# A rational activation's denominator as (|h| + c)|h| in one operation, its scale moved to where sums leave PSUM, and a new order of issue

## The chip, the core and the metric

One core of a Trainium2 chip runs the whole program in one launch. The core has TensorE (PE; its loads of weights are listed as PEld), VectorE (DVE), ScalarE (ACT) and GpSimd (POOL), each with its own row of instructions that it works off in order, and SyncE (SP), which issues the DMAs. SBUF holds operands, PSUM takes the sums of matmuls. The metric is the device time of the core in microseconds (us), the median of several runs.

## The reference

Windowed attention with block summaries, then a network with a rational activation, then a second network (relu6):

```python
def _attn_ref(q, k, v):            # 2 batches, 8 heads, 768 positions, 64 wide
    k_sum = k.reshape(B, H, nb, block, D).max(axis=3)       # block 32
    v_sum = v.reshape(B, H, nb, block, D).mean(axis=3)
    scores_l = scale * np.matmul(q, k.transpose(0, 1, 3, 2))
    mask_l = np.abs(pos[:, None] - pos[None, :]) < window   # 16
    scores_s = scale * np.einsum('bhsd,bhnd->bhsn', q, k_sum) + np.log(block)
    ...                                                     # softmax over both, times v and v_sum

def _moe_ref(x, w_in, w_out, a, b):   # 1536 x 512, 512 x 2048, 2048 x 512
    h = x @ w_in
    P = a[0] + a[1] * h + a[2] * h2 + a[3] * h3
    Q = 1.0 + np.abs(b[0]) * np.abs(h) + np.abs(b[1]) * h2
    g = P / (Q + 1e-06)
    return g @ w_out

def _moe2_ref(x, w_in, w_out):
    h = x @ w_in
    return (h * np.clip(h + 3.0, 0.0, 6.0) / 6.0) @ w_out
```

## The kernel before

**Stages.** The attention runs in twelve groups of 128 positions (six for each batch). A group has scores on PE (`L507`), which DVE takes out of PSUM with the mask and a running extreme (`L520`), the exponential on ACT (`L534`), sums (`L538`), a guard (`L546`), a reciprocal (`L552`), the share (`L549`, `L555`), transposes on PE (`L574`) that are copied out by ACT or DVE (`L577`, `L578`), the product with v (`L591`), and two halves of its result for the first network: a rounded one (`L601`, `L602`) and the rest (`L603`, on DVE). `L376` on DVE forms the block maxima of k; `L432` and `L434` form the block means of v on PE.

The first network takes 1536 positions as three chunks of 512 and the 2048 inner columns as two halves of eight slices of 128, that is 48 steps. A step is a first product (`L637`, twelve matmuls, since each operand is a rounded part and a rest), the activation `act1`, a `low` operation (`L745`, the rest of g) and a second product (`L654`, twelve matmuls into the four banks y_81 to y_84). The first sixteen steps are single, 512 columns wide, and lie beside the attention's second half; the other thirty-two run in sixteen pairs, 1024 wide. After eight steps `evac` takes the four sums out of PSUM (`L667` on ACT or `L668` on DVE the first time, `L672` the second). The second network follows (`L812`, `L850`, `L865`, `L939` and others).

**Weights** come in as 512 KB pieces by DMA (`raw`, `L280`), and are brought into a rounded part and a rest by a row of operations on several engines: a clamp (`L305`), ACT (`L309`), a shift (`L311`), an or (`L313`), a cast (`L286` on ACT, `L322` on DVE) and a subtraction (`L325`).

**The activation before.** `act1` puts |h| into q (`L701`, ACT), forms u = |b1||h| + |b0| on POOL, ACT or DVE (`L704`, `L707`), multiplies q by u on POOL or DVE (`L717`), so that q + 1 + 1e-6 is the denominator. The numerator runs on ACT (`L721`) and DVE (`L723`, `L724`). An approximate reciprocal r comes from Ln and Exp on ACT (`L728`, `L730`), is used by `L733`, corrected by `L735` and `L737`, all on DVE; `L739` on ACT rounds the result and `L745` on DVE or POOL forms its rest. u is a single buffer, shared by all steps; in a single step r stands in u, in a pair in PSUM.

**What sets the order.** All operations are recorded in a plan first. Where an operation has forms on several engines, a digit of the string `PICK` chooses. The string `ORDER` then gives one order of all operations, and each engine gets its own in that order; nothing is reordered after that. Where the planner sees PE idle for more than 0.6 us it puts filler matmuls on a bank that is free (`L1045`); at the start sixteen such matmuls on a zero tile z stand in the code (`L349`).

**Names.** hs_91 to hs_94 are four PSUM banks; attention groups from the fifth on have their scores and products in hs_93 and hs_94, and single steps have theirs in hs_91 and hs_92. raw_70 to raw_73 are buffers for raw weights, t_74, t_75, q_76, q_77, u the tiles of the activation (early groups and early weights borrow them), xx_115 and xx_117 chunks of the first network's input, ab the tile of the coefficients a and |b|.

## Time and profile before

| what | value |
|---|---|
| median of 3 runs | 589.26 us (588.09 to 589.53) |
| span of the profiled execution | 587.4 us |
| PE busy | 578.6 us, 98% |
| DVE busy | 494.4 us, 84% |
| ACT busy | 348.5 us, 59% |
| POOL busy | 294.7 us, 50% |
| chain that ended last, on PE | 94% |

The span runs from the first to the last instruction of one execution; the time of a run is 589.26 - 587.4 = 1.86 us longer here. Busy time is what an engine's operations took; an average over the whole says little, so the rows below cut the program into the stretch ahead of the first network (0 to 38 us), the single steps (38 to 150), the pairs (150 to 323) and the second network. In a row of groups the mean time of one operation stands behind the busy time, and then the time that its engine was idle just before it, with what ended most of that. In a chain of waits each piece was waited for by the next.

### The profile page before, as it was taken

Reading aid. Unit: us, or ns where it says so; the run is one execution under the profiler, and the core shown is the slowest. Engines: PE = TensorE matmul, PEld = TensorE weight load, DVE = VectorE, ACT = ScalarE, POOL = GpSimd, SP = SyncE. Lnnn points to the kernel's source line nnn. Section 1 sums busy time; section 2 is a strip of 40 time slices with the busy share of each in tenths; the row PEclk is TensorE's granted clock in tenths of the full one; section 3 lists DMA queues with packets and bytes.
Section 4 is the critical chain, followed back from the end, with each engine's and each line's share of the span. In section 5 each row is a group of like instructions: output and inputs, shape, how many; then the busy total and the mean of one; then the engine's idle time right before and its main releaser. Section 6 shows DMA issues by size and latency. Waiting matters only on the chain.

```text
span 587.4 us, 9645 instructions
## 1 busy us (share of the span) xinstructions
PE 578.6 (98%) x3608; PEld 466.6 (79%) x3613; DVE 494.4 (84%) x887; ACT 348.5 (59%) x648; POOL 294.7 (50%) x272
## 2 busy tenths in 40 slices
PE   8999999999999999999999999999999999999997
PEld 4477788888888888888888888888888888888886
DVE  5999999999989898988899998968687786866643
ACT  3988998988676677658657455524540434424410
POOL 1777676573475657654766472131423175523210
PEclk9999999999999999999999999999999999999999
DMA  8986534301222223110000141320313023002005
GB/s 311 352 306 209 192 118 151 104 30 35 73 71 73 76 101 110 37 36 2 17 20 1 37 143 37 107 73 0 144 32 113 1 73 126 18 0 73 1 1 214
DMA packets 17983, 53.10 MB, mean 90 GB/s; under 512 B 2273, under 2 KB 2785, under 8 KB 17937
## 3 DMA queue, kind: packets, MB, share of 16 engines
q1 hardware_dynamic: 17936, 52.49, 26.1%
q8 instruction: 28, 0.46, 0.3%
q14 instruction: 19, 0.15, 0.1%
HBM read 48.55 MB, written 3.15 MB: 88 GB/s over the span
## 4 chain that ended last, share of the span: by engine, by line
PE 94%; DMA 2%; DVE 1%; SPq 1%; issue 1%; POOL 0%; ACT 0%; DVEq 0%
PE y L654 23%; PE y L850 22%; PE hb L637 15%; PE hc L812 13%; PE hs L637 8%; PE hc L939 7%; PE hs L591 2%; PE hs L507 2%; PE hs L574 1%; DMA mask_sb<-in_masks 1%; DMA k<-in_blk 1%; SPq L280 1%; DVE s L520 0%; POOL s L549 0%; PE hs L434 0%
## 5 line engine op out<-in xcount | busy, mean ns | idle before, releaser
L654 PE MATMUL y<-g,wt 128*128 128x512 f32 x576 | 139.1, 392 | 0.0
L654 PEld LDWEIGHTS y<-g,wt 128*128 128x128 f32 x576 | 106.8, 188 | 22.3 <-POOL g L745 0.3
L850 PE MATMUL y<-wt,g 128*128 128x512 f32 x480 | 116.1, 389 | 0.0
L850 PEld LDWEIGHTS y<-wt,g 128*128 128x128 f32 x480 | 90.1, 188 | 18.7
L637 PE MATMUL hb<-xx,wt 128*128 128x512 f32 x384 | 89.5, 389 | 0.0
L325 POOL TENSOR_TENSOR wt<-raw,wt 128x512 fp32r<-128x512 f32 x44 | 62.4, 1425 | 51.0 <-DVE wt L322 30.4
L637 PEld LDWEIGHTS hb<-xx,wt 128*128 128x128 f32 x384 | 72.1, 188 | 15.0
L309 ACT ACTIVATE raw<-raw 128x512 f32<-128x512 f32 x62 | 41.1, 676 | 33.3 <-POOL raw L305 24.6
L717 POOL TENSOR_TENSOR q<-q,u 128x512 f32<-128x512 f32 x34 | 46.2, 1368 | 23.8 <-ACT u L707 14.4
L828 POOL TENSOR_TENSOR g<-t,g 128x512 fp32r<-128x512 f32 x17 | 23.4, 1380 | 63.3 <-ACT g L825 63.3
L825 ACT ACTIVATE g<-t 128x512 fp32r<-128x512 f32 x40 | 25.0, 628 | 49.4 <-PE y L850 43.4
L305 POOL TENSOR_SCALAR raw<-raw 128x512 f32<-128x512 f32 x44 | 35.8, 815 | 34.1 <-DMA raw<-in_w 33.9
L286 ACT ACTIVATE wt<-raw 128x512 fp32r<-128x512 f32 x56 | 36.8, 671 | 25.7 <-POOL raw L796 6.6
L313 DVE SCALAR_TENSOR_TENSOR raw<-raw 128x512 int32<-128x512 int32 x62 | 47.7, 779 | 4.3 <-ACT raw L309 4.1
L637 PE MATMUL hs<-xx,wt 128*128 128x512 f32 x192 | 47.8, 398 | 0.0
L812 PE MATMUL hc<-wt,wt 128*128 128x512 f32 x192 | 47.4, 389 | 0.0
L745 POOL TENSOR_TENSOR g<-t,g 128x512 fp32r<-128x512 f32 x22 | 30.6, 1397 | 30.3 <-ACT g L739 25.8
L939 PE MATMUL hc<-xx,wt 128*128 128x512 f32 x192 | 45.6, 389 | 0.0
L865 DVE SCALAR_TENSOR_TENSOR part<-y,part 128x512 f32<-128x512 f32 x36 | 24.4, 684 | 22.1 <-PE y L850 22.0
L939 PEld LDWEIGHTS hc<-xx,wt 128*128 128x128 f32 x192 | 36.0, 188 | 7.5
L812 PEld LDWEIGHTS hc<-wt,wt 128*128 128x128 f32 x192 | 36.0, 188 | 7.5
L637 PEld LDWEIGHTS hs<-xx,wt 128*128 128x128 f32 x192 | 35.1, 188 | 7.7 <-issue 0.2
(175 smaller groups left out, 1097.6 us busy)
## 6 DMA issues: line engine op xcount, KB each, us to landing
raw<-in_w SPq DMA_DIRECT2D x62, 512.0 KB, 4.2
vv<-in_vw SPq DMA_DIRECT2D x6, 512.0 KB, 7.1
out<-part SPq DMA_DIRECT2D x12, 256.0 KB, 2.9
k<-in_kT SPq DMA_DIRECT2D x4, 384.0 KB, 3.7
q<-in_qT SPq DMA_DIRECT2D x6, 256.0 KB, 7.5
e<-in_kT SPq DMA_DIRECT2D x4, 384.0 KB
raw<-in_vt SPq DMA_DIRECT2D x3, 512.0 KB, 5.1
e<-in_vw SPq DMA_DIRECT2D x3, 512.0 KB
```

Source lines behind the costliest of these rows:

```text
L286: nc.scalar.activation(out_, in_, AF.Copy)
L305: eng.tensor_scalar(out=hif, in0=hif, scalar1=CAP, scalar2=-CAP, op0=ALU.min, op1=ALU.max)
L309: add(ACT, 0.58, lambda: nc.scalar.activation(hif, hif, AF.Prelu, scale=REBIAS, alpha=2.0 ** 32), [kr], [(kr, 1)])
L313: add(DVE, 0.61, lambda: nc.vector.scalar_tensor_tensor(out=lo, in0=hi, scalar=3, in1=lo, op0=ALU.logical_shift_left, op1=ALU.bitwise_or), ...
L325: eng.tensor_tensor(out=to()[:, 1], in0=src, in1=to()[:, 0], op=ALU.subtract)
L637: mm(ps, lt, rt, start=(k == 0), stop=(k == 11))
L654: mm(y, lt, rt, start=(i == 0 and j == 0), stop=(i == HALF - 1 and j == 2))
L717: eng.tensor_tensor(out=q2[a][:, w], in0=q2[a][:, w], in1=u2[:, w], op=ALU.mult)
L745: eng.tensor_tensor(out=g2[a][:, 1, w], in0=t2[a][:, w], in1=g2[a][:, 0, w], op=ALU.subtract)
L812: mm(bank_at(bank_), left(lp, kk), right(rp, kk), start=(j == 0), stop=(j == 5))
L850: mm(yb[d], lt, rt, start=(j == 0 and e == 0), stop=(j == QUART - 1 and e == 2))
L939: mm(bank_at(2 * a + u), w_at(n)[:, lp, kk * P:(kk + 1) * P], x_of(2)[:, rp, kk, :], start=(j == 0), stop=(j == 11))
```

## The change

The denominator 1 + 1e-6 + |b0||h| + |b1|h^2 is written as |b1| times (C1/|b1| + (|h| + c)|h|) with c = |b0|/|b1|. So one scalar_tensor_tensor on DVE that reads q through both inputs, (q + c) q, takes the place of `L704` and `L717`; on POOL it is a pair, an addition into u and a product. The factor 1/|b1| goes to the sums: the first `evac` copies scale by -1/|b1|, the second's scalar is -1/|b1| in place of -1. Columns of ab hold c, C1/|b1|, the scale of Ln, the bias of Exp and -1/|b1|; six operations of one column each on DVE (`prepare`), an Ln on ACT and one more addition on DVE make them, early on.

```diff
-    ab = pool.tile([P, 8], F32, name="ab")
+    ab = pool.tile([P, 16], F32, name="ab")
...
-            val = (C1, -float(60.0 * np.log(2.0)), 3.0, C1 * LNS)[b]
+        for b, val in ((2, 3.0), (3, C1 * LNS)):
...
+        add(ACT, 0.12, lambda: nc.scalar.activation(ab[:, 12:14], ab_in[:, 4:6], AF.Abs), ["abi2"], ["ab2"])
+        def prepare():
+            ts(out=col(8), in0=col(13), scalar1=TINY, scalar2=None, op0=ALU.max)
+            nc.vector.reciprocal(out=col(9), in_=col(8))
+            ts(out=col(6), in0=col(8), scalar1=LNS, scalar2=None, op0=ALU.mult)
+            ts(out=col(4), in0=col(12), scalar1=col(9), scalar2=None, op0=ALU.mult)
+            ts(out=col(5), in0=col(9), scalar1=C1, scalar2=None, op0=ALU.mult)
+            ts(out=col(10), in0=col(9), scalar1=-1.0, scalar2=None, op0=ALU.mult)
+        add(DVE, 0.9, prepare, (), ["ab2"])
+        add(ACT, 0.25, lambda: nc.scalar.activation(ab[:, 7:8], ab[:, 8:9], AF.Ln), ["ab2"], ["ab3"])
...
-            add(ACT, 0.48, lambda: nc.scalar.copy(part_of(c)[:, d, :], y), yk, pk + old,
+            add(ACT, 0.5, lambda: nc.scalar.activation(part_of(c)[:, d, :], y, AF.Copy, scale=ab[:, 10:11]), ["ab2", *yk], pk + old,
...
-                out=pt, in0=y, scalar=-1.0, in1=pt, op0=ALU.mult, op1=ALU.subtract), yk, pk)
+                out=pt, in0=y, scalar=ab[:, 10:11], in1=pt, op0=ALU.mult, op1=ALU.add), ["ab2", *yk], pk)
...
-        lins = [(POOL, us_of(0.73, 1.17), lambda: lin(nc.gpsimd), True), (ACT, us_of(0.71, 1.15), lin_a, False),
-                (DVE, us_of(0.46, 0.73), lambda: lin(nc.vector), True)]
...
-            def times(eng, w=w):
-                eng.tensor_tensor(out=q2[a][:, w], in0=q2[a][:, w], in1=u2[:, w], op=ALU.mult)
...
+            def times(w=w):
+                nc.vector.scalar_tensor_tensor(
+                    out=q2[a][:, w], in0=q2[a][:, w], scalar=ab[:, 4:5], in1=q2[a][:, w], op0=ALU.add, op1=ALU.mult)
+            def times_p(w=w):
+                nc.gpsimd.tensor_scalar(out=u2[:, w], in0=q2[a][:, w], scalar1=ab[:, 4:5], scalar2=None, op0=ALU.add)
+                nc.gpsimd.tensor_tensor(out=q2[a][:, w], in0=q2[a][:, w], in1=u2[:, w], op=ALU.mult)
+            add(DVE, 0.61, times, ["ab2"], [("q", a, w), ("u", w)], port=True, more=[(POOL, 2.0, times_p, True)])
...
-            r(), q, AF.Ln, scale=LNS, bias=lnb[:, 3:4]), qk + ["lnb"], rk)
+            r(), q, AF.Ln, scale=ab[:, 6:7], bias=lnb[:, 3:4]), qk + ["lnb", "ab2"], rk)
...
 PICK = (
-    '0000230000000000001100111010000000011100001100000000000001000000110000000101110000001010000000000010'
+    '0001230011121100000001111000000111101100000000000000101000000110010000010001001000000000000000000001'
```

`PICK` and `ORDER` are new as a whole, and the code's lines move: line numbers of after are 18 higher from the functions of the attention on (`L376` is `L394`, `L520` is `L538`, `L603` is `L621`), and 11 higher in the rest of `act1` (`L723` is `L734`, `L724` is `L735`, `L733` is `L744`, `L735` is `L746`, `L745` is `L756`); the new operation on DVE is `L724` of after. Three places show what moved.

SP at the program's start, before and then after (k, q, v: operands of the attention, in_w: weights):

```order
L280 DMA k_95<-in_kT 128x768 x4
L280 DMA q_96<-in_qT 128x512
L298 DMA raw_70<-in_w 128x1024
L280 DMA mask_sb<-in_masks 128x360
L280 DMA q_96<-in_qT 128x512
L298 DMA raw_71<-in_w 128x1024
L280 DMA e_98<-in_blk 64x192
L280 DMA q_96<-in_qT 128x512
L298 DMA t_75<-in_w 128x1024
```

```order
L280 DMA k_95<-in_kT 128x768 x4
L298 DMA raw_71<-in_w 128x1024
L280 DMA q_96<-in_qT 128x512
L280 DMA e_98<-in_blk 64x192
L280 DMA mask_sb<-in_masks 128x360
L280 DMA q_96<-in_qT 128x512 x2
L280 DMA id_sb<-in_ident 128x128
L298 DMA raw_73<-in_w 128x1024
L298 DMA raw_72<-in_w 128x1024
```

The first piece of weights stands ahead of the first q, and the second and third q stand one behind the other; in_bv, which holds b, is SP's 13th row after and its 29th before.

DVE around the last results of the first four groups, before and then after (xx_115 is the first chunk; hs_93, hs_94 and y_81 hold the products with v):

```order
L578 COPY t_74<-hs_92 120x512
L311 TENSOR_SCALAR raw_70<-raw_70 128x512
L376 TENSOR_REDUCE ks_66<-e_97 128x24
L311 TENSOR_SCALAR q_77<-q_77 128x512
L603 TENSOR_TENSOR xx_115<-hs_93,xx_115 128x4x128
L376 TENSOR_REDUCE ks_66<-e_97 128x24
L603 TENSOR_TENSOR xx_115<-y_81,xx_115 128x4x128
L305 TENSOR_SCALAR raw_71<-raw_71 128x512
L603 TENSOR_TENSOR xx_115<-hs_94,xx_115 128x4x128
L603 TENSOR_TENSOR xx_115<-hs_93,xx_115 128x4x128
L313 SCALAR_TENSOR_TENSOR q_77<-q_77 128x512
```

```order
L311 TENSOR_SCALAR q_77<-q_77 128x512
L596 COPY t_74<-hs_91 120x512
L596 COPY t_74<-hs_92 120x512
L465 COPY vv_99<-hs_94 24x512
L621 TENSOR_TENSOR xx_115<-hs_93,xx_115 128x4x128
L394 TENSOR_REDUCE ks_66<-e_97 128x24 x2
L621 TENSOR_TENSOR xx_115<-hs_94,xx_115 128x4x128
L621 TENSOR_TENSOR xx_115<-hs_93,xx_115 128x4x128
L313 SCALAR_TENSOR_TENSOR q_77<-q_77 128x512
L621 TENSOR_TENSOR xx_115<-y_81,xx_115 128x4x128
L311 TENSOR_SCALAR raw_71<-raw_71 128x512
```

The subtraction from y_81 now stands behind those from hs_93 and hs_94, a copy of a block mean (`L465`) has come to DVE, and a clamp and a shift of raw weights have left this piece. The six column operations of `prepare` stand just ahead of it.

DVE in the first single step, before and then after:

```order
L723 TENSOR_TENSOR t_75<-t_75,hs_91 128x512
L578 COPY pt_108<-hs_93 120x512
L724 SCALAR_TENSOR_TENSOR t_75<-t_75,ab,hs_91 128x512
L704 TENSOR_SCALAR u<-q_77,ab 128x512
L602 CAST xx_117<-hs_93 128x4x128
L723 TENSOR_TENSOR t_75<-t_75,hs_92 128x512
L311 TENSOR_SCALAR raw_71<-raw_71 128x512
L603 TENSOR_TENSOR xx_117<-hs_93,xx_117 128x4x128
L724 SCALAR_TENSOR_TENSOR t_75<-t_75,ab,hs_92 128x512
L733 SCALAR_TENSOR_TENSOR t_75<-t_75,ab,u 128x512
L552 RECIPROCAL stat_69<-stat_69 128x4
L735 SCALAR_TENSOR_TENSOR u<-q_77,u 128x512
```

```order
L734 TENSOR_TENSOR t_75<-t_75,hs_91 128x512
L735 SCALAR_TENSOR_TENSOR t_75<-t_75,ab,hs_91 128x512
L724 SCALAR_TENSOR_TENSOR q_77<-q_77,ab 128x512
L394 TENSOR_REDUCE ks_66<-e_97 128x24
L386 TENSOR_SCALAR ab<-ab 128x1
L394 TENSOR_REDUCE ks_66<-e_97 128x24
L734 TENSOR_TENSOR t_75<-t_75,hs_92 128x512
L570 RECIPROCAL stat_69<-stat_69 128x4
L621 TENSOR_TENSOR xx_117<-hs_93,xx_117 128x4x128
L735 SCALAR_TENSOR_TENSOR t_75<-t_75,ab,hs_92 128x512
L744 SCALAR_TENSOR_TENSOR t_75<-t_75,ab,u 128x512
L746 SCALAR_TENSOR_TENSOR u<-q_77,ab,u 128x512
```

`L704` has become the new operation on q_77, the rounding `L602` and a copy of the transposes have left, and two block maxima have come between.

## Rows read from the trace of the kernel before

**Rows 1.** The page's busy times: us, share of the span, instructions.

```profile
PE 578.6 (98%) x3608; PEld 466.6 (79%) x3613; DVE 494.4 (84%) x887; ACT 348.5 (59%) x648; POOL 294.7 (50%) x272
```

**Rows 2.** Windows: us, busy us of each engine, granted clock, DMA share, GB/s.

```profile
0.00:38.00 38.00, 33.69 (x470) 18.37 (x474) 30.76 (x112) 27.57 (x80) 21.84 (x37) 1.00 0.95 334
38.00:150.00 112.00, 111.09 (x1226) 89.55 (x1228) 107.17 (x287) 102.57 (x267) 73.86 (x73) 1.00 0.38 124
150.00:323.00 173.00, 173.00 (x765) 143.15 (x764) 157.76 (x177) 116.43 (x134) 106.42 (x86) 1.00 0.16 52
323.00:584.00 261.00, 260.81 (x1151) 215.50 (x1149) 198.14 (x314) 101.91 (x170) 92.61 (x78) 1.00 0.19 65
...
38.00:54.00 16.00, 15.42 (x242) 12.21 (x247) 14.53 (x51) 14.03 (x45) 12.20 (x15) 1.00 0.73 246
54.00:71.00 17.00, 16.76 (x239) 13.64 (x232) 16.66 (x44) 15.91 (x36) 10.85 (x12) 1.00 0.52 158
```

**Rows 3.** Chain of waits: start us, us, what.

```profile
21.45 6.15 DMA k<-in_blk
```

**Rows 4.** Timeline of PE: start us, us, engine, line, operation, [idle before <-releaser].

```profile
6.93 1.67 PE L1045 MATMUL hs<-z 128*128 128x512 bf16 x7
8.90 0.40 PE L507 MATMUL y<-k,q 64*64 64x96 f32 x8 [0.29 <-DMA q<-in_qT]
...
36.46 1.03 PE L1045 MATMUL hs<-z 128*128 128x512 bf16 x4 [0.16 <-issue]
...
38.72 0.40 PE L507 MATMUL hs<-k,q 64*64 64x96 f32 x8
```

**Rows 5.** Timeline of DVE, the same columns.

```profile
10.62 0.28 DVE L520 CUSTOM_DVE_ANT_0 s<-y,mask_sb 128x120 f32<-128x120 f32 x1 [1.51 <-DMA mask_sb<-in_masks]
...
36.71 1.27 DVE L603 TENSOR_TENSOR xx<-hs,xx 128x512 fp32r<-128x512 f32 x2
```

**Rows 6.** Groups by form on DVE, 38 to 150 us: count, busy us, mean ns, idle before.

```profile
L735 DVE SCALAR_TENSOR_TENSOR u<-q,u 128x512 f32<-128x512 f32 x14 | 10.4, 745 | 0.3
...
L313 DVE SCALAR_TENSOR_TENSOR raw<-raw 128x512 int32<-128x512 int32 x12 | 8.7, 742 | 0.0
...
L745 DVE TENSOR_TENSOR g<-t,g 128x512 fp32r<-128x512 f32 x9 | 7.4, 821 | 0.0
...
L717 DVE TENSOR_TENSOR q<-q,u 128x512 f32<-128x512 f32 x5 | 3.9, 772 | 0.0
...
L552 DVE RECIPROCAL stat<-stat 128x4 f32<-128x4 f32 x16 | 2.6, 170 | 0.6 <-POOL stat L546 0.4
L578 DVE COPY pt<-hs 120x512 f32<-120x512 f32 x3 | 2.1, 688 | 1.7 <-PE hs L574 1.7
...
L538 DVE TENSOR_REDUCE stat<-s 128x4 f32<-128x480 f32 x2 | 1.3, 648 | 0.1
L704 DVE TENSOR_SCALAR u<-q,ab 128x512 f32<-128x512 f32 x1 | 1.2, 1222 | 0.0
L546 DVE TENSOR_SCALAR stat<-stat 128x4 f32<-128x4 f32 x3 | 1.2, 398 | 0.0
...
L305 DVE TENSOR_SCALAR raw<-raw 128x512 f32<-128x512 f32 x1 | 0.4, 417 | 0.0
```

**Rows 7.** Single lines, 38 to 150 us: duration ns min/median/max, first and last start us.

```profile
L735 DVE SCALAR_TENSOR_TENSOR u<-q,u x14: 679/691/1506, 54.6 to 145.1; 128x512 f32<-128x512 f32 x14
...
L717 POOL TENSOR_TENSOR q<-q,u x11: 1287/1303/1739, 49.0 to 147.5; 128x512 f32<-128x512 f32 x11
...
L704 POOL TENSOR_SCALAR u<-q,ab x13: 772/780/1573, 48.2 to 146.7; 128x512 f32<-128x512 f32 x13
```

**Rows 8.** Groups by form on DVE, 0 to 38 us, columns of rows 6.

```profile
L311 DVE TENSOR_SCALAR raw<-raw 128x512 int32<-128x512 int32 x6 | 3.2, 539 | 0.0
...
L322 DVE CAST wt<-t 128x512 fp32r<-128x512 f32 x1 | 0.4, 426 | 0.0
```

More of the change, by code (lines that the diff above doesn't have):

```diff
@@ L33 @@
 LNS = 2.0 ** -60
+TINY = 2.0 ** -60
 REBIAS = 2.0 ** -112
@@ L368, in consts3 @@
         add(ACT, 0.12, lambda: nc.scalar.copy(ab[:, 0:4], ab_in[:, 0:4]), ["abi"], ["ab"])
-        add(ACT, 0.12, lambda: nc.scalar.activation(ab[:, 4:6], ab_in[:, 4:6], AF.Abs), ["abi2"], ["ab2"])
+        add(ACT, 0.12, lambda: nc.scalar.activation(ab[:, 12:14], ab_in[:, 4:6], AF.Abs), ["abi2"], ["ab2"])
+        def prepare():
+            col = lambda n: ab[:, n:n + 1]
+            ts = nc.vector.tensor_scalar
+            ts(out=col(8), in0=col(13), scalar1=TINY, scalar2=None, op0=ALU.max)
[6 more added lines that the diff above has]
+        add(ACT, 0.25, lambda: nc.scalar.activation(ab[:, 7:8], ab[:, 8:9], AF.Ln), ["ab2"], ["ab3"])
+        add(DVE, 0.15, lambda: nc.vector.tensor_scalar(
+            out=ab[:, 7:8], in0=ab[:, 7:8], scalar1=float(np.log(LNS)), scalar2=None, op0=ALU.add), (), ["ab3"])
     def keys(b):
@@ L666, in evac @@
             old = [("v", "b"), ("v", "c")] if c == 0 else [("k", 1, p) for p in range(4)] + [("vs", 0), ("vs", 1), ("vs", 2), ("vs", 3), ("s", 3)]
-            add(ACT, 0.48, lambda: nc.scalar.copy(part_of(c)[:, d, :], y), yk, pk + old,
-                more=[(DVE, 0.6, lambda: nc.vector.tensor_copy(part_of(c)[:, d, :], y), False)])
+            add(ACT, 0.5, lambda: nc.scalar.activation(part_of(c)[:, d, :], y, AF.Copy, scale=ab[:, 10:11]), ["ab2", *yk], pk + old,
+                more=[(DVE, 0.61, lambda: nc.vector.tensor_scalar(
+                    out=part_of(c)[:, d, :], in0=y, scalar1=ab[:, 10:11], scalar2=None, op0=ALU.mult), False)])
         else:
@@ L735, in act1 @@
         add(DVE, us_of(0.61, 1.14), lambda: nc.vector.scalar_tensor_tensor(
-            out=r(), in0=q, scalar=C1, in1=r(), op0=ALU.add, op1=ALU.mult), qk, rk, port=not two)
+            out=r(), in0=q, scalar=ab[:, 5:6], in1=r(), op0=ALU.add, op1=ALU.mult), qk, rk, port=not two)
         add(DVE, us_of(0.61, 1.14), lambda: nc.vector.scalar_tensor_tensor(
```

112 lines of the change are left out of this document (50 added, 62 removed).

## The prediction

> **What bounds the kernel now.** I read the busy times first [rows 1]: PE is busy in 98% of the span, DVE in 84%, POOL in half. Then the table by stage [rows 2]. From 38 to 150 us, while the sixteen single steps of the first network run beside the rest of the attention, PE is busy 111.09 of 112 us and DVE 107.17. From 150 to 323 PE is busy in all 173.00 and DVE in 157.76, and from 323 to 584 PE in 260.81 of 261 and DVE in 198.14. The granted clock is 1.00 in every stage, the level of 2.4 GHz. So behind 38 us PE sets the time, and no operation that leaves DVE, ACT or POOL there can shorten it by more than PE's own gaps, 0.91 + 0.00 + 0.19 us. The change removes no useful matmul.
>
> Ahead of 38 us things are otherwise. The chain of waits passes through a DMA that lands at 21.45 + 6.15 = 27.60 [rows 3], with the DMA engines 0.95 busy [rows 2]. Then the PE timeline [rows 4] shows four filler matmuls from 36.46 for 1.03 us, to 37.49, and the scores of the fifth attention group only at 38.72, 1.23 later. They write the PSUM banks hs_93 and hs_94, which the pair of `L603` on DVE has read by 36.71 + 1.27 = 37.98 [rows 5]. Two views of this stretch therefore matter: how much of it the fillers take, and what DVE has to do before that pair.
>
> The end of the program, the last output tiles and their write, is untouched. The profiled execution's span is 587.4; the median of the runs, 589.26, is 1.86 more, and I carry that difference over.
>
> **Part 1, the denominator in the stage that DVE could bound (38 to 150 us).** Before, a single step spends one `L704` (13 on POOL at 780 ns median, one on DVE at 1222, two on ACT) and one `L717` (11 on POOL at 1303, five on DVE at 772 mean) [rows 6, 7]. After, twelve of the sixteen are one new operation on DVE and four are a pair on POOL. No row shows the new operation. The nearest is `L735`, which is also a scalar_tensor_tensor with one scalar and two SBUF inputs of 128x512: 745 ns mean, 679 at least, 1506 at most [rows 6, 7]. I take 745. The chosen engines of the `low` step change too, so two `L745` (821) leave DVE. This part gives DVE 12 x 0.745 - 5 x 0.772 - 1.222 - 2 x 0.821 = +2.2 us.
>
> The rewritten order and choice of engines add more between the `L603` that frees hs_93 and the end of the sixteenth single step: six `L305` at 417 (+2.50), five `L322` at 426 (+2.13), four `L546` at 398 (+1.59), one subtraction `L325` at the 679 minimum of a two-input operation (+0.68); three reductions or scalings like `L538` at 648 (-1.94), two `L578` at 688 (-1.38) and one `L602`, taken at half of the pair of `L603` (-0.64), leave; an `L311` against an `L313`, and two scaled copies in place of two plain ones, I put at nothing since both sides are of one size [rows 5 to 8]. That sums to +2.9, so DVE has 2.2 + 2.9 = +5.1 us in a stage in which it is idle 112 - 107.17 = 4.83 us. Against that POOL loses 13 x 0.780 + 11 x 1.303 and gains 4 x (0.780 + 1.303) and about three `L745` of its own, taken at its `L717`: -12.2 us of its 73.86. Records of one DVE form vary: the mean of `L735` stands 745 - 691 = 54 ns over its median [rows 6, 7]. If the 40 records of `L735`, `L717`, `L313` and `L745` all do (2.2 us) and this shrinks with POOL's load, 12.2 / 73.86 of it is 0.4 us. Net: +4.7 us of work against 4.83 of idle.
>
> Is the idle usable? Of it, 1.7 us stand ahead of `L578` [rows 6], of which two of three leave DVE, and 0.6 ahead of `L552`, mostly for an `L546` on POOL, which comes to DVE. These 2.3 us I count as usable. The remaining 4.7 - 2.3 = 2.4 us must find room in the other 2.5. The tightest place is early: up to the `low` of the third single step the same count gives DVE +2.2 us, and from 38 to 71 us it is idle 1.47 + 0.34 = 1.81 [rows 2]. So some 0.4 us are over there, which the slack between `low` and the second product covers or not. I take **+0.5 us**. Bounds: 0 (all covered; PE's gap of 0.91 in this stage closed would give -0.9) and +5.1 (no idle time usable, no shorter records).
>
> The Trainium skill speaks against this part: "SBUF — State Buffer", section "Who interferes with whom", says that a DVE instruction with two SBUF inputs contends with a GpSimd instruction that reads SBUF, and that the later one fully blocks. The new operation reads |h| through both inputs, like the `L735` whose longest record is 1506. The trace agrees that such records stretch. What it would come to at its worst is rival (c).
>
> **Part 2, the way to 38.7 us.** DVE is dense there, so its work ahead of the pair of `L603` counts. By the order of both kernels: less one `L305`, one `L311` and one `L578` (0.42 + 0.54 + 0.69), more one `L313`, one cast, one copy, one `L538`, two `L546`, one scaling of that reduction's size, and six column operations for 1/|b1| and c, each taken at the 0.17 of `L552` (0.74 + 0.43 + 0.69 + 0.65 + 0.45 + 0.65 + 1.02) [rows 6, 8]: +3.0. One `L603` (0.64) and one `L313` (0.74) of this count now stand behind the operation that frees the scores' banks, so +1.6 counts. The six small operations wait for |b|, whose DMA is 13th on SP's queue after and 29th before; behind them on DVE stand the reciprocals, the turn copies and then the `L603`. If |b| came late all of these would wait, but 13 of SP's rows land well ahead of the row that lands at 27.6 [rows 3], and DVE meets the small operations behind the last scores of the first four groups.
>
> The start moves too. DVE's first `L520` waits 1.51 us for the mask until 10.62 [rows 5]. After, an `L311` and an `L313` of the first raw weights (0.54 + 0.74 = 1.3 us) stand ahead of it and fit into that wait: -1.3. But a weight DMA of 512 KB now stands ahead of the first q on SP, and 30 warming matmuls stand ahead of the first scores instead of 23. Seven of them took 1.67 us, and the scores started at 8.90, 0.30 behind them [rows 4]; with seven more they start at 10.3 at the earliest, and the first `L520` can start near 10.7 to 11.7. I take +0.4 (bounds 0.1 and 1.1). Sum of part 2: 1.6 - 1.3 + 0.4 = **+0.7 us**. Bounds: +2.7 when the early idle hides nothing (1.6 + 1.1), and below nothing -2.4, when the stretch from 36.30, where the fillers' idle time of 0.16 begins, to 38.72 closes: in the order after, no filler stands between the values and the fifth group's scores, and six and six stand earlier.
>
> **Part 3, everything behind 150 us.** The pair steps send 12 more half operations to DVE and fewer to POOL, and drop 16 `L704`. At 0.75 to 0.82 us each that is under 10 us on an engine that is idle 15.2 us there [rows 2]; PE is without a gap in all 173 us and its own matmuls are unchanged. The 1/|b1| in the copies out of PSUM replaces copies one for one. **0**, and the bound is what a late `low` could cost, at most the 0.5 us of part 1 again.
>
> **Sum.** 587.4 + 0.7 + 0.5 + 0 = 588.6 span, plus 1.86: about **590.4 us**. About 0.3% (1.8 us) is what a measurement of this kernel can tell from no change, so this is within it, on its upper side.
>
> **Rivals.** (a) *The gap ahead of 38.7 closes.* For it: the order puts the values' last banks and the `L603` of hs_93 and hs_94 ahead of the one of y_81, so DVE frees the scores' banks earlier in its row, and the DMA bytes ahead of the 27.6 landing are equal. Against it: DVE's +1.6. With -2.4 and nothing in the singles the time is 586.9; with half of it, 588.1. (b) *DVE becomes the bound in the single steps (slower).* Place: the singles from 38 to 150 us. Price: the work over the idle time. It decides as soon as less than 4.7 us of DVE's 4.83 can be used. With 2.4 us unusable and part 2 as summed the time is 587.4 + 0.7 + 2.4 + 1.86 = 592.4; with none usable, and part 2 at its bound, 587.4 + 2.7 + 5.1 + 1.86 = 597.1. (c) *The new operation collides with POOL each time.* At 1506 instead of 745 each, 12 of them cost 9.1 us more, so 587.4 + 0.7 + 9.1 + 1.86 = 599.1; one `L735` in fourteen was that long, though, and POOL has a sixth less to do. This is the rule of the Trainium skill's "SBUF — State Buffer", "Who interferes with whom", at its strongest. (d) *Nothing moves*, since PE is dense and the early edits cancel: 589.3.
>
> **How the numbers follow.** My forecast with (d), from 587.5 to 591.0: 0.44. (a): 0.19. (b): 0.34. (c): 0.03. Faster by over 0.3% needs 1.8 of the 3.3 us that PE has idle or filled between 36.3 and 150, which is (a) nearly whole: 0.19. Slower: (b) and (c), 0.37. The range leaves out a tenth on each side: from 586.9, the whole of (a), to 594.0, past the middle of (b).
>
> **What would show it.** In the profile after: the first `L637` near 40.7 instead of 40.0 (under 39 speaks for (a)); PE still without a gap behind 150; DVE at 111 to 112 of the 112 us of the single steps; no second product on PE's list of waits with more than 0.5 us (2 us or more speaks for (b)); new operations at 0.68 to 0.75 us, a longer mean speaks for (c). If |b| came late, DVE would show a wait at the small operations. The prediction is wrong if the stage to 38.7 changes by more than 2.7 us either way, or if pieces behind 150 are no longer dense.

## The result and the profile after

The changed kernel takes 598.12 us (median of 4 runs, 596.8 to 598.7), beside 589.39 us for the kernel before on the same chip: 1.0141 of its time, 95% interval 1.0121 to 1.0162. It is slower by about 8.7 us, and above the forecast's range. The profiled execution's span is 596.9 us, 9.5 more than 587.4. The page's busy times, and the shares of the chain that ended last:

```profile
PE 584.6 (98%) x3621; PEld 468.4 (78%) x3621; DVE 506.1 (85%) x918; ACT 342.4 (57%) x643; POOL 271.6 (45%) x244
...
PE 74%; DVE 15%; ACT 4%; issue 3%; POOL 2%; DMA 1%; SPq 0%; ACTq 0%; DVEq 0%
```

PE is still busy in 98% [rows 1], but PE held 94% of the chain before and holds 74% now; DVE, ACT and POOL have 21% of it. The table by stage, columns as in [rows 2]:

```profile
0.00:38.00 38.00, 33.83 (x357) 16.43 (x359) 27.10 (x113) 23.72 (x72) 13.79 (x28) 0.91 0.83 295
38.00:150.00 112.00, 111.24 (x1344) 90.78 (x1339) 109.48 (x304) 103.28 (x278) 50.12 (x49) 1.00 0.42 137
150.00:323.00 173.00, 170.63 (x747) 139.56 (x747) 161.92 (x183) 106.73 (x120) 101.71 (x79) 1.00 0.16 52
323.00:584.00 261.00, 259.55 (x1144) 214.23 (x1143) 203.52 (x313) 108.12 (x176) 105.96 (x90) 1.00 0.17 57
```

Three things differ. Ahead of 38 us the granted clock is 0.91 instead of 1.00, and PE has 357 records there instead of 470. The single steps are as dense as before (111.24 against 111.09). Behind 150 us PE is no longer without gaps: 2.37 us idle to 323 instead of 0.00, then 1.45 instead of 0.19.

By the starts of the products the program is 4.6 us late at the first product of the first network (44.53 against 39.97). The single steps give 1.0 us of that back. From the first product to the start of the 341st matmul of the products, when both kernels have the whole attention behind them, it is 109.27 us before and 108.30 after (before first, columns as in [rows 2]):

```profile
39.97:149.24 109.27, 108.76 (x1165) 87.59 (x1160) 104.44 (x283) 100.54 (x263) 73.00 (x72) 1.00 0.37 123
```

```profile
44.53:152.83 108.30, 108.02 (x1165) 87.43 (x1159) 106.29 (x300) 98.93 (x268) 47.67 (x45) 1.00 0.39 125
```

From there to the last matmul it loses 5.9 us: 4.95 us in seven stops of 0.23 to 1.77 us, and most of the rest at the matmul behind each stop, which the next one follows after 0.34 us instead of 0.23. (The table shows less idle time than that, since the ends of matmuls are modelled.) 4.6 - 1.0 + 5.9 = 9.5 us, the difference of the spans.

**Ahead of 38 us**, PE's timeline of after, columns as in [rows 4]:

```profile
11.24 0.40 PE L525 MATMUL y<-k,q 64*64 64x96 f32 x8 [0.55 <-DMA q<-in_qT]
...
15.51 0.25 PE L525 MATMUL y<-ks,q 64*64 64x24 f32 x5
18.19 0.19 PE L525 MATMUL y<-ks,q 64*64 64x24 f32 x1 [2.43 <-issue]
18.32 1.89 PE L349 MATMUL hs<-z 128*128 128x512 bf16 x4
...
44.53 1.65 PE L655 MATMUL hs<-xx,wt 128*128 128x512 f32 x6
```

The first scores start at 11.24, not 8.90 [rows 4]. Then, amid the scores of the third group, behind PE's 449th record, PE stands still for 2.43 us, for nothing that the trace of semaphores shows ("issue"). The matching rows of before, behind its 447th record, with its first product, and then the DMA queues of the two kernels around the stop (before first; queue: packets, MB, share):

```profile
15.40 0.25 PE L507 MATMUL y<-ks,q 64*64 64x24 f32 x4
16.12 0.24 PE L507 MATMUL y<-ks,q 64*64 64x24 f32 x2 [0.47 <-issue]
...
39.97 1.20 PE L637 MATMUL hs<-xx,wt 128*128 128x512 f32 x4
```

```profile
q8 instruction: 1, 0.02, 5.4%
```

```profile
q8 instruction: 1, 0.02, 5.2%
```

Each kernel has one transfer of instructions there, 16 KB: under way from 13.60 to 14.73 before, from 15.56 to 16.65 after. PE goes on 1.4 to 1.5 us behind its landing in both. That fits a PE that has run out of instructions, though no semaphore in the trace names the wait; before, the stop took 0.5 us, now 2.4. What follows is in windows of 2 us (the clock stands behind POOL's column):

```profile
16.00:18.00 2.00, 0.00 (x0) 0.00 (x0) 1.73 (x14) 2.00 (x8) 1.19 (x4) 0.81 0.97 302
18.00:20.00 2.00, 1.81 (x6) 0.59 (x5) 1.90 (x5) 2.00 (x11) 0.72 (x1) 0.50 1.01 310
...
22.00:24.00 2.00, 2.00 (x9) 1.66 (x8) 0.13 (x1) 0.34 (x1) 1.51 (x4) 0.50 1.04 420
```

After the stretch in which PE did nothing, the granted clock is 0.50, the level of 1.2 GHz, from 17.25 to 24.07 us. Four fillers of `L349` took 1.89 us at it.

**Behind 150 us**, PE's waits of after (150 to 597 us: total, times, longest; before has none there):

```profile
PE hb L655 <- DVE t L748: 2.3, 4, 1.6
PE y L672 <- POOL g L756: 1.2, 1, 1.2
PE y L861 <- DVE g L839: 0.2, 1, 0.2
```

The longest can be followed through the timelines of after, here POOL, then ACT, DVE and PE:

```profile
169.49 1.58 POOL L728 TENSOR_SCALAR u<-q,ab 128x512 f32<-128x512 f32 x1 [2.20 <-ACT q L720]
171.15 1.30 POOL L729 TENSOR_TENSOR q<-q,u 128x512 f32<-128x512 f32 x1
172.44 1.57 POOL L728 TENSOR_SCALAR u<-q,ab 128x512 f32<-128x512 f32 x1
174.09 1.29 POOL L729 TENSOR_TENSOR q<-q,u 128x512 f32<-128x512 f32 x1
```

```profile
175.41 1.21 ACT L739 ACTIVATE hb<-q,lnb,ab 128x1024 f32<-128x1024 f32 x1 [0.36 <-POOL q L729]
176.66 1.09 ACT L741 ACTIVATE hb<-hb,ab 128x1024 f32<-128x1024 f32 x1
```

```profile
178.61 1.27 DVE L744 SCALAR_TENSOR_TENSOR t<-t,ab,hb 128x1024 f32<-128x1024 f32 x1
179.80 1.28 DVE L746 SCALAR_TENSOR_TENSOR hb<-q,ab,hb 128x1024 f32<-128x1024 f32 x1
181.00 0.74 DVE L724 SCALAR_TENSOR_TENSOR q<-q,ab 128x512 f32<-128x512 f32 x1
181.66 1.22 DVE L748 SCALAR_TENSOR_TENSOR t<-hb,t 128x1024 f32<-128x1024 f32 x1
```

```profile
182.93 2.33 PE L655 MATMUL hb<-xx,wt 128*128 128x512 f32 x9 [1.61 <-DVE t L748]
```

POOL starts both halves' pairs as soon as ACT has |h|, and needs 174.09 + 1.29 - 169.49 = 5.9 us; the logarithm (`L739`) waits for it, the exponential and DVE's correction follow, one of the new operations (`L724`, for the next pair) stands in DVE's row between them, and PE waits 1.61 us for the bank. The addition of that pair, `L728`, is the surprise (ns, least, median, most; first and last start):

```profile
L728 POOL TENSOR_SCALAR u<-q,ab x15: 1558/1576/2115, 54.4 to 328.0; 128x512 f32<-128x512 f32 x15
```

```profile
L729 POOL TENSOR_TENSOR q<-q,u x15: 1287/1299/1617, 56.1 to 329.7; 128x512 f32<-128x512 f32 x15
```

`L704`, a multiplication and an addition in one, took 780 on the same engine and shape [rows 7]; this addition alone takes twice that, and is slower than a product of two tensors.

### The profile page after: what moved, and what is told of

The parts are those of the page before. It is cut to its first block, busy times and chain, and to the rows that moved or that the text cites. A ratio compares the mean times of both kernels' runs of the same rounds, so it can differ in the third digit from the quotient of the medians.

```text
span 596.9 us, 9663 instructions
## 1 busy us (share of the span) xinstructions
PE 584.6 (98%) x3621; PEld 468.4 (78%) x3621; DVE 506.1 (85%) x918; ACT 342.4 (57%) x643; POOL 271.6 (45%) x244
## 4 chain that ended last, share of the span: by engine, by line
PE 74%; DVE 15%; ACT 4%; issue 3%; POOL 2%; DMA 1%; SPq 0%; ACTq 0%; DVEq 0%
PE y L861 22%; PE hc L823 13%; PE y L672 11%; PE hs L655 8%; PE hc L950 7%; PE hb L655 5%; DVE t L735 2%; DVE hb L746 2%; DVE t L744 2%; PE hs L592 2%; PE hs L609 2%; DVE q L724 2%; DVE t L734 2%; PE hs L525 2%; DVE t L748 1%
## 5 line engine op out<-in xcount | busy, mean ns | idle before, releaser
L325 POOL TENSOR_TENSOR wt<-raw,wt 128x512 fp32r<-128x512 f32 x43 | 58.8, 1370 | 85.4 <-ACT wt L286 45.0
L655 PE MATMUL hb<-xx,wt 128*128 128x512 f32 x384 | 91.2, 391 | 2.3 <-DVE t L748 2.3
L655 PEld LDWEIGHTS hb<-xx,wt 128*128 128x128 f32 x384 | 71.8, 188 | 18.8 <-DVE t L748 4.0
L839 POOL TENSOR_TENSOR g<-t,g 128x512 fp32r<-128x512 f32 x23 | 31.9, 1394 | 79.8 <-ACT g L836 79.8
L309 ACT ACTIVATE raw<-raw 128x512 f32<-128x512 f32 x62 | 41.1, 673 | 38.7 <-POOL raw L305 34.7
L305 POOL TENSOR_SCALAR raw<-raw 128x512 f32<-128x512 f32 x42 | 33.0, 790 | 36.3 <-DMA raw<-in_w 32.8
L756 POOL TENSOR_TENSOR g<-t,g 128x512 fp32r<-128x512 f32 x24 | 33.9, 1418 | 32.0 <-ACT g L750 25.8
L655 PE MATMUL hs<-xx,wt 128*128 128x512 f32 x192 | 47.8, 397 | 0.0
L286 ACT ACTIVATE wt<-raw 128x512 fp32r<-128x512 f32 x45 | 29.9, 670 | 27.9 <-DVE raw L313 14.7
L655 PEld LDWEIGHTS hs<-xx,wt 128*128 128x128 f32 x192 | 35.1, 188 | 7.5
L311 DVE TENSOR_SCALAR raw<-raw 128x512 int32<-128x512 int32 x62 | 35.1, 578 | 5.0 <-DMA raw<-in_w 4.8
```

The costliest lines, as they stand in the source:

```text
L305: eng.tensor_scalar(out=hif, in0=hif, scalar1=CAP, scalar2=-CAP, op0=ALU.min, op1=ALU.max)
L309: add(ACT, 0.58, lambda: nc.scalar.activation(hif, hif, AF.Prelu, scale=REBIAS, alpha=2.0 ** 32), [kr], [(kr, 1)])
L311: add(DVE, 0.34, lambda: nc.vector.tensor_single_scalar(lo, lo, 29, op=ALU.logical_shift_right), [kr], [(kr, 0)], port=True)
L325: eng.tensor_tensor(out=to()[:, 1], in0=src, in1=to()[:, 0], op=ALU.subtract)
L655: mm(ps, lt, rt, start=(k == 0), stop=(k == 11))
L756: eng.tensor_tensor(out=g2[a][:, 1, w], in0=t2[a][:, w], in1=g2[a][:, 0, w], op=ALU.subtract)
```

## The experiments

My theories after the result: the 4.6 us ahead of the first product come from the late instructions, by the stop or by the clock that falls behind it; the 5.9 us behind 150 come from the denominators themselves, POOL's long pair and DVE's twelve more halves. The rivals: the new order is at fault in both places, not the operations; or the number of operations on DVE is, whatever POOL does.

**1. The fillers ahead of the third group's scores, 1 or 7.** After stands them at 1, before at 7.

```diff
+        idle[third] = (("h", 0), 7)     # after_fill6; before_nofill6: 7 -> 1
```

> The changed kernel with seven filler matmuls ahead of the third group's scores where it has one (the kernel before has seven there). In the changed kernel TensorE stops for 2.43 us inside these scores, after its 449th record, and its granted clock is then 0.50 from 17.3 to 24.1 us. Theory F (it stops because its own next instructions come late: a 16 KB instruction fetch lands at 16.65 there, 14.73 in the kernel before): the stop falls again near the 449th record, so some 12 records earlier in the program, and is under 1.5 us; if the clock then stays at 1.00, the first L637 comes at 41 to 42 us in place of 44.6 and the time is about 595. Theory D (these scores wait for data or a bank): the stop ends at the same matmul at the same 18.2 us, 1.4 us shorter, and the first L637 comes no earlier than 42.

> The kernel before with one filler matmul ahead of the third group's scores in place of seven. Theory F (TensorE runs out of instructions when it gets to its 449th record too early): the stop of 0.68 us grows to 1.5 us or more at about the same count of records; if the clock falls to 0.50 behind it, the first L637 comes 2 to 4 us later than 40.0, and the time is 591 to 593. Theory O (the stop belongs to the new order of DMAs and not to the fillers): no stop above 1 us, clock 1.00, the time within 1 us of 589.3.

after_fill6: 596.17 us, 1.0124 (1.0104 to 1.0144). PE's timeline and a window:

```profile
18.12 0.31 PE L525 MATMUL y<-ks,q 64*64 64x24 f32 x7 [1.68 <-issue]
18.36 1.04 PE L349 MATMUL hs<-z 128*128 128x512 bf16 x4
...
41.95 1.43 PE L655 MATMUL hs<-xx,wt 128*128 128x512 f32 x5
```

```profile
18.00:20.00 2.00, 1.88 (x15) 1.00 (x15) 1.90 (x3) 2.00 (x11) 0.60 (x1) 1.00 1.06 301
```

With six more fillers in front, the stop stands at a place six matmuls earlier in the work and again behind PE's 449th record. So it belongs to the count of instructions and not to a matmul or its data. It is shorter (1.68, not under the 1.5 expected), the clock stays at 1.00, four `L349` take 1.04 instead of 1.89 us, and the first `L655` comes 2.6 us earlier. In before_nofill6 the expected longer stop did not come: PE waits 0.76 and 0.44 us for DVE ahead of the place, and reaches its 449th record only at 15.93, 1.4 us behind the landing of the instructions at 14.51. The first `L637` came at 38.77, 1.2 us earlier than in before, yet the time is 590.14, 1.0013 (0.9996 to 1.0030): PE then waits inside the single steps, twice for DVE (0.7 and 0.5 us) and 0.8 with nothing shown. Of a gain ahead of 40 us in that order, the single steps took back all.

**2. The first q's earlier on SP's queue, fewer fillers for them.**

```diff
+        seq[at], seq[to] = seq[to], seq[at]              # first q ahead of the first weights
+        idle[score[0]], idle[score[2]] = (("h", 0), 11), (("h", 0), 8)        # after_q_first
+        seq.remove(q3); seq.insert(seq.index(sp_[9]) + 1, q3)                 # after_q_early: one more q early
+        idle[score[0]], idle[score[1]], idle[score[2]] = (("h", 0), 11), (("h", 0), 2), (("h", 0), 7)
```

> The changed kernel with its first q loaded ahead of the first 512 KB of weights (these two DMAs exchanged) and with eleven filler matmuls ahead of the first scores and eight ahead of the third group's, in place of eighteen and one. Up to here three runs agree that TensorE's 449th record is followed by a stop that ends 6.6 to 6.7 us after its 100th record, which comes with the first scores (9.44 to 16.12 us in the kernel before, 11.54 to 18.19 in the changed one). Theory F, with the late first scores as its root: the first scores start near 9.0, the stop ends near 16.2, the clock stays at 1.00, and the first L637 comes at 39.5 to 41 in place of 44.6; time 593.5 to 595. Rival: the fourth group's q, which SP issues at 15.3 us, or the weights hold the rest, so the first L637 stays at 42 or later: 596 or more.

> The changed kernel with all four early q's loaded early (the first ahead of the first weights, the fourth right behind the third, where the changed kernel has it twelve DMAs later) and with 11, 2 and 7 filler matmuls ahead of the first three groups' scores. With only the first q exchanged, the first scores started at 8.5 us, but the third and the fourth group's waited for their q's until 16.4 and 22.8 (14.1 and 16.6 in the kernel before), and the first L637 came at 41.7. Theory: the late q's are the rest of the 4.6 us ahead of the first L637, which then comes at 39.5 to 40.5; time 593 to 594.5. Rival: another row (the weights that are now later, the products with v) holds it at 41 or later: 595.5 or more.

after_q_first: 596.31, 1.0108 (1.0082 to 1.0134). The scores start at 8.49 and the stop is gone (PE comes to the place at 17.75, 1.4 us behind the landing), but the third and fourth groups wait for their q to 16.35 and 22.83. The second group's scores wait 1.79 us for theirs, and behind that wait the granted clock is 0.50 from 11.94 to 15.36: it does not take a stop for instructions. First `L655` at 41.7, near the rival's 42 or later. after_q_early: 596.88, 1.0104 (1.0071 to 1.0137), PE's timeline:

```profile
8.62 0.40 PE L525 MATMUL y<-k,q 64*64 64x96 f32 x8 [0.50 <-DMA q<-in_qT]
...
41.12 1.21 PE L655 MATMUL hs<-xx,wt 128*128 128x512 f32 x4
```

Its instruction transfer runs from 12.8 to 13.96, PE does not stop, the clock is at 1.00. That gives 3.4 of the 4.6 us back, not the 4.0 expected (40.5); place and time are those of the rival, that another row holds the first product at 41 or later. 3.4 us is also what half of full speed loses in the 24.07 - 17.25 = 6.8 us that after spent at it.

**3. The denominators in before's order.** before_newden keeps the order and the engines of before and puts the new forms in the places of `L717` (`L704` is left empty); before_newden21 also gives DVE the 12 singles and 21 of 32 halves of pairs that it has in after; before_times21 instead gives DVE 21 of the halves of before's own product.

```diff
-            add(POOL, 1.26, lambda f=times: f(nc.gpsimd), ..., more=[(DVE, 0.61, lambda f=times: f(nc.vector), True)])
+            add(POOL, 1.26, times_p, ..., more=[(DVE, 0.61, times, True)])    # before_newden; newden21: D or P from a string
+            now = (nc.vector,) if PAIRS[n - SINGLE + w] == "D" else (nc.gpsimd,)   # before_times21, times unchanged
```

> The change proper in the order of the kernel before: (|h| + c)|h| in one operation wherever the product was on DVE (5 of 16 singles, 9 of 32 halves of pairs), an addition and a product where it was on POOL, the scale 1/|b1| moved, the columns made ahead of the first single step; PICK, ORDER and the fillers as before. Theory O (the 9.5 us are the new order's): within 1.5 us of 589.3, first L637 at 40.0. Theory N (the new operation costs them by DVE time or by collisions with POOL): 592 or more, with stops of TensorE between 150 and 330 us.

> The order, fillers and other choices of the kernel before, with the new denominator on DVE in the same twelve singles and 21 halves of pairs as in the changed kernel, and on POOL in the rest (with 5 and 9 on DVE this order took 618.0). Theory O (the new order is what costs the changed kernel its 4.9 us behind 40 us): 590 to 593. Theory N (the new operation costs it in any order): 595 to 605, with TensorE's stops behind 150 us again.

> The kernel before with its own products of the pairs (q times u, two SBUF inputs) on DVE in the 21 halves in which the changed kernel has its new operation there (9 in the kernel before), u made as before; POOL loses 12 x 1.3 us. Theory N (12 more operations of 0.7 us are too much for DVE between 150 and 330 us): 594 to 599. Theory S (the damage is peculiar to the new operation, or to the addition that stands with POOL's product): 589 to 592.

before_newden: 618.0, 1.0487 (1.0462 to 1.0511). Its 34 additions on POOL (columns as in [rows 6]):

```profile
L731 POOL TENSOR_SCALAR u<-q,ab 128x512 f32<-128x512 f32 x34 | 58.2, 1711 | 22.5 <-ACT q L703 8.6 <-ACT t L736 5.4 <-DVE stat L553 2.8
```

So the new forms alone cost more than the whole change: the long addition hurts wherever POOL keeps many of them, and the new choice of engines repairs most of it. before_newden21: 602.59, 1.0218 (1.0193 to 1.0242). before_times21: 598.06, 1.0135 (1.0102 to 1.0168), with PE waiting in the pairs as in after (the two longest of four lines; `L740` is `L737` of before, `L748` its `L745`):

```profile
PE hb L637 <- DVE t L740: 2.5, 4, 1.2
PE y L654 <- DVE g L748: 0.9, 1, 0.9
```

Here no new operation and no long addition exists. Twelve more halves on DVE in before's order cost nearly as much as the change (a span of 593.6 in the profiled execution, 6.2 more than before's). DVE's 15 idle us there [rows 2] are no room for 9 us more.

**4. Other shares between DVE and POOL in after.** In the pairs, 9, 23 and 32 halves on DVE instead of 21.

```diff
+            if two:
+                now = (times, times) if HALVES[n - SINGLE + w] == "D" else (times_p, times_p)
```

> The changed kernel with the product of the pairs on DVE in only 9 of 32 halves, the same ones as in the kernel before, and on POOL in 23 (the changed kernel has 21 and 11). Order and fillers unchanged. Theory N (DVE has too much to do between 150 and 333 us): TensorE's stops of 4.6 us there shrink by half or more, time about 595. Theory O (it is the order of issue, whichever engine does the product): the stops stay or grow, since POOL's pair takes about 2.1 us in place of 0.7: 598 or more.

> The changed kernel with the two products of the last pair on DVE in place of POOL. In the changed kernel POOL works off two additions and two products (325.12 to 331) ahead of the last rest of g, and TensorE stops 1.39 us for it at 331. If that row is the cause: the stop goes, time about 596.8 (-1.3). If DVE is as late there (its chain to 320 us is nearly dense): no gain, 598.

> The changed kernel with all 32 halves of the pairs' products on DVE (21 there, 11 on POOL). Theory N (DVE's work is the bound between 150 and 333 us): 11 x 0.74 = 8 us more for an engine that has 11 us idle there and waits in a row: 600 to 606. Theory P (POOL's two operations of 2.1 us per half, and the rows of DVE that they stretch, are what DVE and TensorE wait for): the stops of 4.6 us shrink, 594 to 596.

after_pairs9: 609.63, 1.0350 (1.0330 to 1.0370); PE waits 9.0 us for `hb` behind DVE, whose own row is emptier (149.46 of 173 us), because ACT's logarithm waits 29.6 us for POOL's products. The time is in theory O's range, but the waits lead to POOL's long pair, now in 23 halves instead of 11, and not to the order. after_last_dve, with the last pair's two halves on DVE: 598.17, 1.0143 (1.0114 to 1.0172). The POOL stop at 331 is gone, 1.0 us of another came at 317, and no gain is left, against the expectation. after_all_dve: 597.05, 1.0121 (1.0095 to 1.0148), PE's waits from 150 to 340 (`L751` is `L748` of after):

```profile
PE hb L655 <- DVE t L751: 2.8, 4, 1.6
PE hc L826 <- ACT q L910: 1.3, 1, 1.3
```

Between the expectations: without POOL's pairs the stops remain, now by DVE. Fewer on DVE is bad, more is no better, so each engine is near its limit in this order.

**5. Each half of the denominator left out in the pairs.** after_skip_dve leaves DVE's 21 halves out, after_skip_pool POOL's 11, so that |h| stands where the denominator should.

```diff
+            add(DVE, 0.61, times if not two else lambda: None, ..., more=[(POOL, 2.0, times_p, True)])    # skip_dve
```

> The changed kernel without the 21 new operations of the pairs on DVE (the pairs' denominators lack a factor there); the 11 pairs of operations on POOL stay. Theory N (DVE's time): TensorE's stops of 4.95 us behind 160 us fall under 1 us, 593 to 594. Theory O (the order of issue): they stay, 597 to 598.

> The changed kernel without the 11 additions and products of the pairs on POOL (the pairs' denominators lack a factor there); the 21 new operations on DVE stay. Theory C (collisions with POOL's two operations stretch DVE's rows, 17.1 us over their shortest between 152 and 332 us): the stops halve, 595 to 596. Theory N (DVE's own time): the stop of 1.39 us at 331 goes, the others stay: 596.5 to 597.

592.62, 1.0039 (1.0020 to 1.0058), and 593.27, 1.0048 (1.0031 to 1.0065). The windows from 150 to 323 (skip_dve, then skip_pool):

```profile
150.00:323.00 173.00, 173.00 (x765) 143.11 (x764) 153.46 (x166) 109.67 (x123) 102.19 (x83) 1.00 0.16 52
```

```profile
150.00:323.00 173.00, 172.35 (x756) 141.28 (x755) 160.96 (x184) 108.40 (x121) 72.69 (x62) 1.00 0.16 52
```

Either brings nearly all, which the expectation of the second run missed: with DVE's halves gone a stop by POOL at 326 is nearly all that is left (1.0 us), with POOL's gone 1.1 us in small ones. With 21 halves on DVE the stops need both, POOL's late product and DVE's additional operation in the same chain; with all 32 there (after_all_dve) DVE alone makes them.

**6. POOL's addition as two operations.** Column 11 of ab is 1, so that the same sum is formed as 1 x |h| + c.

```diff
-                nc.gpsimd.tensor_scalar(out=u2[:, w], in0=q2[a][:, w], scalar1=ab[:, 4:5], scalar2=None, op0=ALU.add)
+                nc.gpsimd.tensor_scalar(out=u2[:, w], in0=q2[a][:, w], scalar1=ab[:, 11:12], scalar2=ab[:, 4:5], op0=ALU.mult, op1=ALU.add)
```

> The changed kernel with POOL's addition |h| + c written with two operations (times a column of ones, plus c), as the old u = |b1||h| + |b0| was. In the changed kernel the one-operation addition takes 1576 ns median on POOL (15 of them), the old two-operation form took 780. Theory T (the form is slow, and it is the mis-sized part of the price): it takes about 0.78 us here, POOL has 12 us less to do, TensorE's stops of 4.95 us behind 160 us fall to 2 to 3.5, time 595 to 597. Rival (any addition into u by POOL takes that long beside the busier DVE): it stays near 1.5 us and the time near 598.

592.68, 1.0030 (1.0008 to 1.0051), under the 595 to 597 expected. Its addition and its stage (lines are one higher than in after):

```profile
L729 POOL TENSOR_SCALAR u<-q,ab x15: 772/777/1297, 51.0 to 320.2; 128x512 f32<-128x512 f32 x15
```

```profile
150.00:323.00 173.00, 172.88 (x761) 142.22 (x760) 161.03 (x183) 109.75 (x123) 96.81 (x83) 1.00 0.15 52
```

More work in one instruction takes half the time, 777 ns instead of 1576. The two pairs of the chain above get 1.6 us shorter, as much as PE waited there, and the stops behind 150 all but vanish: by the starts of the products the loss there falls from 5.9 to 1.1 us. By the medians it is 5.4 of the change's 8.7 us, a part of which is the clock of the runs (below). The clamp `L305`, also two operations on 128x512, takes 790 ns on POOL in after. Whether it is the number of operations that decides, or the addition as the first of them, was not tried apart. The profiled execution kept the clock at 1.000 and its span was 588.4. PE stopped there too at 449 records, for 1.69 us, but with the clock at 1.00 its first product came at 41.14, as early as in after_q_early without any stop (`L526` and `L656` are `L525` and `L655` of after):

```profile
17.32 0.18 PE L526 MATMUL y<-ks,q 64*64 64x24 f32 x1 [1.69 <-issue]
...
41.14 3.01 PE L656 MATMUL hs<-xx,wt 128*128 128x512 f32 x12
```

So it is the fall of the clock behind the stop, not the stop, that costs the 3.4 us. Five more runs, alike in PE's order up to the first product, bear this out. In after_all_dve, after_pairs9, after_skip_dve and after_skip_pool the stop was about as long as in after (2.15 to 2.50 us), but the clock was at 0.50 for 3.41 us only, and the first product came at 42.84 to 43.11; in after_last_dve the clock was at 0.50 for 6.83 us, as in after, and it came at 44.50. Of the ten runs of after_pool_two three kept the clock (1.00 over the run) and took 589.87 to 590.71; seven lost some (0.994 to 0.997) and took 592.31 to 594.23. The fall of the clock thus comes in some executions of one program. The medians of the two sets lie 593.17 - 590.22 = 2.9 us apart; six of the seven were at 0.997, which is 0.003 x 590 = 1.8 us of clock, and what the rest comes from is not traced. Of after's own four runs none kept it: 0.994 in the one traced, 0.997 in the others.

The same line in before's order, with the shares of before_newden and of before_newden21:

> The change proper in the order of the kernel before, products on the engines as before (618.0 with POOL's one-operation addition), with POOL's addition in two operations. Theory T: 34 additions are 0.79 us shorter, 27 us of POOL's time, and most of the 28 us over the kernel before go: 594 to 602. Rival (the new order of dependence, |h| to the product without u on ACT, costs it): 610 or more.

> The change proper in the order of the kernel before with the products on the changed kernel's engines (602.6), POOL's addition in two operations. Theory N and T together (12 more operations on DVE cost 5 to 6 us as in the old form, 598.1; the rest is POOL's slow addition): 597 to 599.5. Rival: 602 or more.

602.24, 1.0217 (1.0158 to 1.0276), and 601.42, 1.0190 (1.0158 to 1.0222). Of before_newden's loss more than half is gone, of before_newden21's little: the first still has 34 pairs on POOL, the second DVE's twelve halves, and in before's order the single steps lose too (PE busy 105.95 and 106.68 of 112 us). The first came out just above what I expected, the second between the two expectations. Behind 38 us the new order is no culprit, then: with the same engines for the denominators and the same short addition, before's order takes 601.42 and after's, with its other choices of engines, 592.68. Ahead of 38 us it is one: there only the order of loads and fillers had to move for the stop to go (experiment 2).

**7. Both repairs, and one for the rest.** after_q_two joins 2's early q's and 6. after_scores3 also sets the fourth group's scores ahead of the first transposes (moved there, they overwrite a bank that DVE still has to read, so a part of the values differs; the work is the same).

```diff
+        seq.remove(pe_[10]); seq.insert(seq.index(pe_[6]), pe_[10])      # after_scores3
```

> Both mends together: the q's loaded early with fillers 11, 2, 7 (first L637 at 41.1), and POOL's addition in two operations. If the two losses are apart: the sum of the gains, 593 to 595.5; still over the kernel before, since TensorE has no gap there that the change could fill.

> The kernel with both mends (early q's, POOL's addition in two operations; 591.27, first L637 at 41.1), with the fourth group's scores moved ahead of the transposes of the first group, where the kernel before has them, and without the six fillers there. If these late scores hold DVE's row and the softmax of the fourth group: the first L637 comes at 39.5 to 40.3 and the time is 589.3 to 590.3, level with the kernel before. If POOL's and DVE's rows hold it: 41.1 and 591.3 again. It can't be far under the kernel before, since TensorE has no gap behind 60 us in either.

after_q_two: 591.27, 1.0014 (0.9998 to 1.0029), under the 593 to 595.5 expected and no more to be told from before; first product at 41.13. after_scores3: 591.09, 1.0025 (1.0013 to 1.0036), its first product at 42.2, later and not earlier. PE now waits at the transposes (`L593`) for POOL, DVE and ACT, 1.1, 0.8 and 0.7 us. So the last 1.1 us ahead of the first product (41.1 against 40.0) are not PE's queue of scores; PE's waits point at the rows of the softmax on three engines, and which of them decides stays open. No version beats before.

## Why the prediction was wrong

**What bounds the kernel** was read rightly, PE behind 38 us, and the early stretch apart. The removed work could bring nothing there, and brought nothing.

**Part 1 (single steps), +0.5 forecast, -1.0 measured.** The mechanism held, with other sizes: DVE's added work found room. PE came out about as far ahead as the -0.9 that I had named for its gap closed, but its idle time over the same work fell only from 0.51 to 0.28 us, and where the rest came from is not traced. DVE's busy time grew by 109.48 - 107.17 = 2.3 us (1.9 over the same work), not 4.7, though the new operation took 813 ns on average (11 records) and `L746` 831, both more than the 745 taken. POOL lost 23.7 us, twice the 12.2 of the sum, and other records became shorter. The clearest is `L311` (38 to 150 us, before first, columns as in [rows 6]):

```profile
L311 DVE TENSOR_SCALAR raw<-raw 128x512 int32<-128x512 int32 x12 | 8.3, 695 | 0.0
```

```profile
L311 DVE TENSOR_SCALAR raw<-raw 128x512 int32<-128x512 int32 x13 | 6.0, 465 | 0.0
```

The 0.4 us that I allowed for shorter records was the right sign and too small. The Trainium skill's "SBUF — State Buffer", section "Who interferes with whom", counts tensor_scalar among the DVE operations that can contend with GpSimd, in modes that use both of DVE's ports. The trace goes that way, with less of the one and shorter records of the other, but it does not show the mode of `L311`, and that POOL's load is the cause was not tried by itself.

**Part 2 (to 38.7 us), +0.7 forecast, bounds -2.4 and +2.7; measured +4.6.** Here a step was missing. I counted DVE's row and took 10.3 us as the earliest start of the first scores, with 0.4 us for it; they came at 11.24. The term that decided stands in no engine's row, and I had put nothing for it: PE stopped at a fixed place in its count of records, until 1.5 us after a transfer of instructions had landed, and then ran at half the clock to 24.07. With the clock kept the first product came at 41.14, 1.2 late, within the part's bounds and near its 0.7. The trace of before held the sign of it, the 0.47 of "issue" at 16.12, which I passed over.

**Part 3 (behind 150 us), 0 forecast; measured +5.9.** Two terms failed. The POOL pair was priced in part 1 by `L704` at 0.78 + 1.30 = 2.1 us [rows 7] and took 1.58 + 1.30 = 2.9: the row was of the right engine and shape but of another form, and part 3 put nothing for the wait of the logarithm for two such pairs. And the added operations on DVE were held against 15.2 us of idle time in the whole stage. Idle time spread over 173 us is not slack at each step; in a tight stretch (columns as in [rows 2], before first, after behind it) DVE has 2.5 us left before and less than one after:

```profile
150.00:183.00 33.00, 33.00 (x147) 27.32 (x146) 30.49 (x36) 22.33 (x29) 19.39 (x17) 1.00 0.29 97
```

```profile
150.00:183.00 33.00, 31.39 (x139) 25.64 (x138) 32.16 (x37) 21.42 (x28) 20.15 (x15) 1.00 0.19 63
```

The first stop, of 1.61 us, falls at its end. Experiments 5 and 6 show both terms at work: either without the other costs little in after's order. With the addition at the price that I had put on it and the clock kept (the traced run of after_pool_two), the span is 588.4, and the sum had said 588.6. That is luck in part, since its errors cancel: part 2 then measured +1.2, part 1 -1.3, part 3 +1.1.

**The rivals.** (a) did not come: the first product was later, not earlier. (b) named an engine that did become short of room, but in the wrong stage, the single steps, which stayed dense. (c) gave 599.1, nearest to the time, by a mechanism that is not there: the new operation in the pairs (the stretch 150 to 335) is short but for single records,

```profile
L724 DVE SCALAR_TENSOR_TENSOR q<-q,ab x22: 736/744/1403, 152.3 to 317.4; 128x512 f32<-128x512 f32 x22
```

and its price, taken from `L735`'s 745, was right there. (d) fell with parts 2 and 3. Both of the signs that I had named as proof against the forecast appeared: the early stretch off by more than 2.7 us, and products behind 150 no longer dense.

## What to carry to other kernels

Price an operation by a row of its own form, the number of its arithmetic steps included; where no row of that form exists, the range must hold twice the price of the nearest, and the chain through the slower engine has to be drawn to the matmul that waits for it. An engine's idle time in a long stage is no measure of what can be added to it: take the tightest stretch and the order in its row. And where a profile shows PE idle for nothing ("issue") in its first microseconds, look for a transfer of instructions there, and for the granted clock behind it, before moving work ahead of it.
